# A recurrent attention with an MoE layer behind it: another kernel with its own list schedule in place of the scheduled one

## The chip, the cores and the metric

One core of a Trainium2 chip runs the whole program. The metric is the device time of one execution in microseconds (us), the median of several. The five engines are TensorE (PE), VectorE (DVE), ScalarE (ACT), GpSimd (POOL) and SyncE (SP), which here only issues DMAs.

## The reference

Thirty-two sequences (4 batches of 8 heads) of 768 tokens with 40 channels each go through a recurrence, and the joined heads (320 channels) through a layer norm and two dense layers with a ReLU between them.

```
for t in range(S):                            # S = 768, D = 40
    y[t] = r[t] @ state
    Sa = state @ a[t]
    state = state * w[t] - outer(Sa, b[t])
    state = state + outer(v[t], k[t])
x  = y as (4, 768, 320)
xn = (x - mean) / sqrt(var + 1e-6) * g_ln
out = x + relu(xn @ w_ch1) @ w_ch2            # 320 -> 1280 -> 320
```

`w` lies between 0.85 and 0.95. All is float32; the dense weights come as float64.

## The kernel before

The sequence is cut into 24 chunks of 32 tokens. Within a chunk the recurrence becomes matrix products: the decays are folded into `a`, `b`, `k`, `r` by running products, a 32x32 triangular matrix per sequence is inverted, and one small product per sequence carries the 40x40 state to the next chunk. Each chunk has these steps (names and lines of the kernel):

- `prep` (L141 to L195): two scans over a 104-partition tile (L149, L153) give the running products, `a`, `b` and `k` are multiplied by them (L160, L165, on DVE for the first six chunks and on POOL later), 32 products (L178) give the triangular matrices, and DVE signs them out of PSUM (L183). They go to DRAM (`d_g`), because the inversion wants another layout.
- `invert` (L197) and `invert2` (L226): for a slab of two or four chunks, one matrix per partition, DVE does forward substitution. `invert` inverts all 32 rows at once, 60 instructions per slab (L208, L211); `invert2` inverts two 16-row blocks side by side in 28 (L241, L245), and the off-diagonal part is then applied by products (`solve2`, L258). The first three slabs use `invert2`, the other five `invert`. The result goes to DRAM (`d_tt`) and comes back per chunk (`load_tt`).
- `load_cl` (L310): the same running products once more in the token-row layout, by scans of their own (L321, L325), transposed on DVE (L329, L331); POOL then scales `k` and `b` (L339).
- `chain` (L365): the products with the state (L372), the solve (L349 or L258, evacuated by L352 and L362), the products that make the next state (L384), and four multiplications out of PSUM (L390).
- `state`, `post` (L395, L409): transposes on PE (L401, L416) with copies by ACT (L407, L421), products (L429), masks (L435), products (L443), and the output row tile `xt` (L447). One L447 ends the attention of one chunk.
- `norm` (L557) and `moe` (L593): per pair of chunks (256 tokens) ten slices of 128 hidden units. A slice is eight matmuls of 256 columns (L615), a ReLU by ACT (L618), a remainder by DVE (L619), and six matmuls of 320 columns (L601). Each float32 operand is split in a high and a low part.
- `weights` (L456): the float64 words of the dense weights are turned into float32 by ACT, DVE and POOL.
- `warm` (L217): 360 matmuls (L221) whose result nobody reads.

Order: the program emits steps in a loop over chunks with boosts and nudges, and a timeline model of the framework chooses the order on DVE and ACT. All DMAs are issued by SP. At the end, a check of the scans' validity decides whether a sequential fallback (L861) runs; it does not run here.

## Time and profile before

| | |
|---|---|
| median of 3 runs | 710.24 us (708.89 to 710.95) |
| profiled execution, its span | 702.6 us |
| PE, DVE, ACT, POOL busy | 579.0, 564.0, 328.7, 291.4 us |
| moved by DMA | 92.35 MB in 158156 packets |

The profiled execution's span runs from its first to its last instruction; it stands 7.6 us below the median, which has the launch around it. Busy times of one engine overlap a little, so group sums can be above the engine's total. Matmuls overlap even more: a matmul that lasts 300 ns in its row may start 120 ns after the one before it, so the rate is read from start to start. In the line of slices each digit is a fortieth of the span, in tenths; PEclk is the TensorE clock that was granted.

### The profile page before, as it was taken

The numbers are of one execution on the slowest core, as the hardware profiler recorded it, in microseconds if no ns is written. First come the engines' busy times: TensorE is split into PE (matmuls) and PEld (weight loads), VectorE is DVE, ScalarE is ACT, GpSimd is POOL, SyncE is SP. The second block draws the span as 40 slices with busy tenths as digits, with TensorE's granted clock in tenths as the row PEclk, the third lists the DMA queues.
The fourth block names the chain that finished last, engine by engine and source line by source line (L and its number), as shares of the span: only waits on it lengthen the run. The fifth ranks groups of instructions, "written<-read, shape, count | busy, mean of one in ns | idle before, by whom it ended". The sixth has DMA issues, their size and how long they took to land.

```text
span 702.6 us, 24730 instructions
## 1 busy us (share of the span) xinstructions
PE 579.0 (82%) x10386; PEld 511.0 (73%) x10386; DVE 564.0 (80%) x1291; ACT 328.7 (47%) x816; POOL 291.4 (41%) x328
## 2 busy tenths in 40 slices
PE   2787778786697879788878889798987899999994
PEld 2686666675586758776757778697776777889994
DVE  8969899899589967899957999788996999764621
ACT  4314664544243445363366356444656255666220
POOL 8606486757514246146505533543133312233000
PEclk9979796868588799899989899999999899999998
DMA  6787977538635467455558653775336435420100
GB/s 176 202 230 206 280 188 182 136 86 198 137 104 144 99 154 161 124 159 134 131 145 177 141 134 94 169 167 122 89 95 116 117 86 119 109 51 16 38 20 22
DMA packets 158156, 92.35 MB, mean 131 GB/s; under 512 B 126504, under 2 KB 136488, under 8 KB 158040
## 3 DMA queue, kind: packets, MB, share of 16 engines
q1 hardware_dynamic: 158040, 90.72, 52.2%
q8 instruction: 83, 1.36, 0.8%
q14 instruction: 33, 0.27, 0.1%
HBM read 72.06 MB, written 18.64 MB: 129 GB/s over the span
## 4 chain that ended last, share of the span: by engine, by line
DVE 45%; PE 26%; DMA 17%; issue 5%; ACT 3%; SPq 2%; POOL 1%; DVEq 0%; POOLq 0%; ACTq 0%
PE ps L615 8%; PE ps L601 7%; DVE yinv L211 6%; DVE ytmp L208 6%; DMA yinv<-d_g 6%; DMA wa<-in_et_dram 4%; DVE x L390 3%; DVE x5s L435 3%; DVE gE L149 3%; DVE qE L153 3%; DVE hl L619 2%; DMA tt<-d_tt 2%; DVE yinv L245 2%; DMA d_tt<-yinv 2%; DVE gC L321 2%
## 5 line engine op out<-in xcount | busy, mean ns | idle before, releaser
L615 PE MATMUL ps<-xh,w 128*128 128x256 f32 x480 | 117.4, 303 | 3.3 <-DVE xl L589 2.3
L601 PE MATMUL ps<-w,hh 128*128 128x320 f32 x480 | 113.4, 330 | 4.9 <-DVE yinv L211 3.6
L618 ACT ACTIVATE hh<-ps 128x256 fp32r<-128x256 f32 x120 | 45.6, 383 | 140.0 <-PE ps L615 130.9
L615 PEld LDWEIGHTS ps<-xh,w 128*128 128x128 f32 x480 | 87.2, 200 | 8.4 <-DVE xl L589 2.6
L601 PEld LDWEIGHTS ps<-w,hh 128*128 128x128 f32 x480 | 79.2, 197 | 8.9 <-ACT hh L618 5.7
L601 PE MATMUL ps<-w,hl 128*128 128x320 f32 x240 | 75.0, 335 | 12.5 <-DVE hl L619 11.9
L619 DVE SCALAR_TENSOR_TENSOR hl<-ps,hh 128x256 fp32r<-128x256 f32 x120 | 49.5, 414 | 43.2 <-ACT hh L618 40.7
L208 DVE TENSOR_TENSOR ytmp<-yinv 128x30 f32<-128x30 f32 (+19 forms) x150 | 61.7, 412 | 26.4 <-DMA yinv<-d_g 24.4
L165 POOL TENSOR_TENSOR bk<-bk,gE 104x1024 f32<-104x1024 f32 x18 | 41.9, 2327 | 91.7 <-DMA bk<-in_et_dram 71.2
L221 PE MATMUL ps<-start,ident 128*128 128x160 f32 x360 | 74.3, 363 | 0.0
L615 PE MATMUL ps<-xl,w 128*128 128x256 f32 x240 | 71.0, 296 | 0.0
L221 PEld LDWEIGHTS ps<-start,ident 128*128 128x128 f32 x360 | 63.4, 232 | 2.3
L211 DVE TENSOR_TENSOR yinv<-yinv,ytmp 128x30 f32<-128x30 f32 (+19 forms) x150 | 61.1, 408 | 2.3
L601 PEld LDWEIGHTS ps<-w,hl 128*128 128x128 f32 x240 | 45.7, 199 | 16.5 <-DVE hl L619 14.9
L615 PEld LDWEIGHTS ps<-xl,w 128*128 128x128 f32 x240 | 48.2, 201 | 0.5
L362 ACT COPY x<-ps_c 32x160 f32<-32x160 f32 x144 | 40.7, 283 | 12.9 <-PE ps_c L357 9.7
L160 POOL TENSOR_TENSOR aT<-wa,qE 104x512 f32<-104x512 f32 x18 | 25.6, 1423 | 50.8 <-DVE qE L153 41.0
L390 DVE TENSOR_TENSOR x<-ps_c,x2s 40x320 f32<-40x320 f32 x92 | 44.7, 486 | 2.1
L384 PE MATMUL ps_c<-x,xk 128*40 128x40 f32 (+1 forms) x1472 | 43.1, 213 | 3.9 <-ACT x L279 2.9
L164 ACT COPY abd<-aT 40x512 f32<-40x512 f32 x48 | 29.6, 616 | 35.4 <-DVE aT L160 19.6
L372 PE MATMUL ps_c<-x,x2s 96*32 96x40 f32 (+1 forms) x1536 | 30.5, 223 | 18.7 <-issue 6.6
L384 PEld LDWEIGHTS ps_c<-x,xk 128*40 128x40 f32 (+1 forms) x1472 | 37.0, 126 | 9.2 <-ACT x L279 3.5
(174 smaller groups left out, 1359.7 us busy)
## 6 DMA issues: line engine op xcount, KB each, us to landing
clt<-in_cl_dram SPq DMA_DIRECT2D x24, 485.5 KB
wa<-in_et_dram SPq DMA_DIRECT2D x20, 422.9 KB
bk<-in_et_dram SPq DMA_DIRECT2D x20, 416.0 KB
d_g<-gk SPq DMA_DIRECT2D x48, 128.0 KB
x<-in_vt_dram SPq DMA_DIRECT2D x48, 128.0 KB
d_a<-aT SPq DMA_DIRECT2D x24, 214.5 KB
vu<-in_vr_dram SPq DMA_DIRECT2D x24, 208.0 KB
x2s<-d_a SPq DMA_DIRECT2D x48, 82.5 KB
```

Of the source, the lines that this page charges most:

```text
L165: (nc.gpsimd if c >= EARLY else nc.vector).tensor_tensor(out=kb, in0=kb, in1=g[R, :, 0:C].unsqueeze(2).broadcast_to([104, 16, 2, C]), op=A ...
L208: nc.vector.tensor_tensor(out=tv, in0=y[0:n, j + 1:, j:j + 1].broadcast_to([n, m, j]), in1=y[0:n, j:j + 1, 0:j].broadcast_to([n, m, j]), o ...
L211: final["inv", si] = nc.vector.tensor_tensor(out=y[0:n, j + 1:, 0:j], in0=y[0:n, j + 1:, 0:j], in1=tv, op=ALU.add)
L221: nc.tensor.matmul(pw[:, 0:w], lhsT=ident, rhs=start0.rearrange("p h t -> p (h t)")[:, 0:w], start=True, stop=True)
L362: nc.scalar.copy(out=dst[:, :, :, j, 0:D], in_=pu[32 * j:32 * j + 32, :, :, hf])
L372: nc.tensor.matmul(prh[32 * q:32 * q + 32, h], lhsT=X2s[RROW[hf], hf, 32 * p:32 * p + 32], rhs=X2[RROW[hf], hf, p, 0:D], start=True, stop= ...
L384: nc.tensor.matmul(pst[r0:r0 + D, h], lhsT=XK[FROW[hf], 1, hf, p], rhs=X2[FROW[hf], hf, p, 0:D], start=True, stop=True)
L390: nc.vector.tensor_tensor(out=X2n[r0:r0 + D, hf, ps, 0:D], in0=pst[r0:r0 + D], in1=pc.unsqueeze(2).broadcast_to([D, 8, D]), op=ALU.mult)
L601: nc.tensor.matmul(po[u], lhsT=l[:, us], rhs=ws[f"w2_{f}"][:, x], start=f == 0 and n == 0, stop=f == 9 and n == 2)
L615: nc.tensor.matmul(ph, lhsT=l, rhs=r, start=n == 0, stop=n == 7)
L618: nc.scalar.activation(out=hh, in_=ph, func=AF.Relu)
L619: nc.vector.scalar_tensor_tensor(out=hl, in0=ph, scalar=0.0, in1=hh.bitcast(F32), op0=ALU.max, op1=ALU.subtract)
```

## The change

It is a rewrite. What is computed and the split in 24 chunks of 32 tokens stay; these are its parts.

- **Order.** Every step is an `Op` with an engine, an assumed duration, a priority and its reads and writes. `Plan.order` simulates the five engines with these durations and emits all instructions in the order that comes out, with `tc.manual_schedule()`; each engine then runs its own in that fixed order. Chain steps have priority -100 + 18c for chunk c, prep -70 + 18c, post -60 + 18c, MoE 400 + 10g for pair g, so MoE comes only where nothing of the attention is ready.
- **One set of scans.** Time runs forward. The token rows of `k`, `b` and of the running products come from PE products with the identity (`KB`, `gY`), not from second scans. Over four chunks (`SPAN`) the running product is not restarted.
- **Inversion.** All slabs (two of two chunks, five of four) invert only 16-row diagonal blocks: 14 steps of two DVE instructions on 128 partitions. The solve is three products (`p1`, `p2`, `p3`) for every chunk.
- **Tiles side by side.** Products with 40 or 64 rows are paired on both halves of the array. PSUM: two pairs of banks for all attention products, two banks for each of the MoE's two layers.
- **MoE tiles 512 wide.** Two slices share one PSUM bank: ReLU and remainder work on 128x512 at a time. The matmuls themselves stay.
- **Norm.** `xt` is only centred before the transposes; the scale by 1/sqrt(var) is applied at the output (`ot`), the root's refinement is on POOL.
- **DMAs.** Inputs and weights are loaded from ACT's queue (w, a, kb, r, dv and two v per chunk); SP does the rest. One tile per input is loaded once.
- No `warm` matmuls.

The diff, cut to its core (removed code is above):

```diff
+RING = dict(w=2, a=6, kb=2, g=2, q=1, gk=6, KB=6, pi=6, VU=2, vt=2, r=2, T=2, N=2, y=2, ST=2, S=1, Z=1, xt=6, xh=2, ...)
+BASE = dict(chain=-100.0, post=-60.0, prep=-70.0, inv=-45.0, load=-90.0, moe=400.0, wts=-20.0)
...
+                    if e == "PE":
+                        if o.mode != mode:
+                            us += 0.09
...
+    def prep(c):
+        load("w", c, ...); load("a", c, ...); load("kb", c, ...)          # ACT queue
+        add(f"st{c}", "DVE", 0.14, ...); add(f"g{c}", "DVE", 1.3, scan ...)
+        add(f"la{c}", "DVE", 0.4, ...);  add(f"q{c}", "DVE", 1.3, scan ...)
+        add(f"kbq{c}", *(("DVE", 1.25) if c < 2 else ("POOL", 2.35)), ...)  # 104x1024
+        add(f"ag{c}", "POOL", 1.43, ...)                                    # 104x512
+        gy = add(f"gY{c}", "PE", 0.30, ..., mode=(64, 128))      # 8 products
+        pg = add(f"pg{c}", "PE", 0.52, ..., mode=(64, 64))       # 32
+        add(f"gk{c}", "DVE", 0.8, ...)                           # 2 x 128x256
+        add(f"dg{c}_{gg}", "SP", ...)                            # to DRAM, gg = 0, 1
+        kt = add(f"KB{c}", "PE", 0.62, ..., mode=(64, 128))      # 16
+        add(f"KBc{c}", "ACT", 0.74, ...)                         # 128x640
...
+    def invert(i):
+            add(f"yl{c}_{bl}", "SP", ...)                        # 16x16 blocks, 64 bytes a row
+        for m in range(1, 15):
+            def step(o, m=m, n=n, S=S):
+                tt(V, tv, y[:, :, 0:m, m:m + 1].broadcast_to(S), y[:, :, m:m + 1, m + 1:16].broadcast_to(S), ALU.mult)
+                tt(V, yv, yv, tv, ALU.add)
+            add(f"td{c}_{bl}", "SP", ...)
...
+    def chain(c):
+        add(f"ld_T{c}", "SP", ...); add(f"ld_N{c}", "SP", ...); add(f"zN{c}", "POOL", 0.3, ...)
+            pr = add(f"pra{c}", "PE", 0.25, ..., mode=(32, 32)); fence(f"prf{c}", pr, k - .1)
+            add(f"prb{c}", "PE", 0.8, prb, ..., mode=(64, 32))   # 64 products with pra
+        add(f"v0{c}", "ACT", 0.43, ...)                          # 128x320
+        p1 = add(f"p1_{c}", "PE", 0.62, ..., mode=(32, 32));  add(f"v1{c}", "ACT", 0.43, ...)
+        p2 = add(f"p2_{c}", "PE", 0.62, ..., mode=(32, 32));  add(f"v2{c}", "DVE", 0.48, ...)
+        for cb in range(2):
+            p3 = add(f"p3_{c}_{cb}", "PE", 0.32, ...)
+            for gg in range(2):
+                add(f"u{c}_{cb}{gg}", "ACT", 0.43, ...)          # 32x320
+            sp = add(f"ST{c}", "PE", 0.62, ..., mode=(64, 64));   add(f"Sa{c}", "DVE", 0.82, ...)  # 104x640
+            if c % SPAN == SPAN - 1: add(f"Sg{c}", "DVE", 0.82, ...)
...
+    def post(c):    # S (16) + Sc, uT (16) + vt, pz (32) + Z (128x512), ya and yb (64) with a fence, xt
+    def norm(c):    # bn, xc, px (2 transposes, 2 products), xh, xl
+    def moe(g):     # 5 x: ph (16 matmuls), hh (128x512, ACT), hl (128x512, DVE), po (12 matmuls); 2 x: ot, st_o
...
+    order = plan.order()
+    with tc.manual_schedule():
+        for o in order:
+            o.fn(o)
```

A `fence` writes one element of a bank on DVE between two groups of products that accumulate in it. The check at the end is seven small DVE instructions and a product behind all else.

## The prediction

> **What bounds the kernel now.** I read the page first (busy time, slices, chain, groups), then windows of the span, then groups by form, then the timeline of PE for rates.

> ```profile
> span 702.6 us, 24730 instructions
> PE 579.0 (82%) x10386; PEld 511.0 (73%) x10386; DVE 564.0 (80%) x1291; ACT 328.7 (47%) x816; POOL 291.4 (41%) x328
> ...
> DVE  8969899899589967899957999788996999764621
> ...
> DVE 45%; PE 26%; DMA 17%; issue 5%; ACT 3%; SPq 2%; POOL 1%; DVEq 0%; POOLq 0%; ACTq 0%
> ...
> L208 DVE TENSOR_TENSOR ytmp<-yinv 128x30 f32<-128x30 f32 (+19 forms) x150 | 61.7, 412 | 26.4 <-DMA yinv<-d_g 24.4
> ...
> L211 DVE TENSOR_TENSOR yinv<-yinv,ytmp 128x30 f32<-128x30 f32 (+19 forms) x150 | 61.1, 408 | 2.3
> ```

> DVE is busy for 564 us, at nine tenths in most slices until late, and it holds 45% of the chain. Two lines of the inversion alone are 61.7 + 61.1 = 123 us of it. The next view counts finished chunks: each L447 is one.

> ```profile
> core 0: us, DVE busy (x), PEclk, DMA share, GB/s
> 0.00:100.00 100.00, 0.48 (x1) 0.88 0.80 218
> 100.00:300.00 200.00, 2.37 (x5) 0.80 0.58 139
> 300.00:600.00 300.00, 6.68 (x14) 0.94 0.54 129
> 600.00:702.00 102.00, 1.95 (x4) 0.97 0.17 41
> ```

> Six chunks in the first 300 us, fourteen in the next 300 (21.4 us each). So the loss has two parts: a start in which DVE must invert, scan and unpack weights while PE has little to do, and a steady pitch of 21.4 us. The same windows with all engines:

> ```profile
> 175.00:200.00 25.00, 19.11 (x268) 16.42 (x271) 16.05 (x40) 7.79 (x20) 11.51 (x14) 0.62 0.63 141
> ...
> 550.00:600.00 50.00, 45.97 (x899) 39.40 (x893) 47.83 (x128) 24.12 (x64) 17.25 (x24) 1.00 0.44 100
> 600.00:650.00 50.00, 48.78 (x872) 43.66 (x876) 28.84 (x70) 31.93 (x85) 14.22 (x22) 1.00 0.24 56
> ```

> At 600 to 650, with the inversions over, DVE falls to 28.84 of 50 us and PE fills the window (48.78): PE is the next bound.

> **The change, part by part. DVE.** Durations:

> ```profile
> L149 DVE TENSOR_TENSOR_SCAN gE<-wa,start 104x528 f32<-104x528 f32 x24 | 32.5, 1352 | 7.3 <-POOL bk L165 3.6 <-DMA wa<-in_et_dram 3.6
> L447 DVE TENSOR_TENSOR xt<-ps_a,pi 128x320 f32<-128x320 f32 x24 | 11.5, 478 | 0.4 <-PE ps_a L443 0.4
> L183 DVE TENSOR_TENSOR gk<-ps_a,sign 128x512 f32<-128x512 f32 x19 | 12.8, 673 | 0.9 <-PE ps_a L178 0.9
> L321 DVE TENSOR_TENSOR_SCAN gC<-clt,start 128x330 f32<-128x330 f32 x24 | 21.1, 880 | 0.0
> L211 DVE TENSOR_TENSOR yinv<-yinv,ytmp 128x108 f32<-128x108 f32 x8 | 2.8, 346 | 0.1
> L211 DVE TENSOR_TENSOR yinv<-yinv,ytmp 128x30 f32<-128x30 f32 x8 | 2.1, 263 | 0.1
> L619 DVE SCALAR_TENSOR_TENSOR hl<-ps,hh 128x256 fp32r<-128x256 f32 x120 | 49.5, 414 | 43.2 <-ACT hh L618 40.7 <-PE ps L601 1.6
> ```

> Per element 128x320 to 128x512 costs (673 - 478)/192 = 1.02 ns, so 104x640 is about 0.80 us. Per chunk of the new kernel: two scans 2.7; three small column operations about 0.6; gk two of 0.41, 0.8; v2, xt, ot three of 0.48, 1.4; Sa 0.8 and a quarter of Sg 0.2; Z 0.67; two fences 0.2; statistics, centring and xl about 1.8 (three to four instructions the size of L447); hl 2.5 of 0.67, 1.7. The inversion is 7 slabs x 28 instructions of 28 to 112 elements, between 0.263 and 0.346, say 0.3: 59 us, 2.5 a chunk. Sum 13.4, times 24 = 322; the weights stay (about 30). So DVE has some 350 us in place of 564: the inversion loses 64 us against L208 and L211 alone, the second scans (L321 and its twin) and their transposes go. Over a span of 540 that is 65%, no bound any more, though in the first 90 us it still is.

> **ACT, POOL, DMA.** ACT:

> ```profile
> L344 ACT COPY xk<-xk 64x640 f32<-64x640 f32 x48 | 34.7, 724 | 3.2 <-POOL xk L339 2.2
> L352 ACT ACTIVATE hbd<-ps_c 32x320 f32<-32x320 f32 x72 | 30.7, 427 | 3.0 <-PE ps_c L372 2.3
> ```
> ```profile
> 609.18 1.98 SPq L307 DMA_DIRECT2D rbd<-in_rd_dram  x2
> ...
> 611.26 0.94 SPq L301 DMA_DIRECT2D x<-in_vt_dram  x2
> ```

> Eight copies of about 0.43 a chunk (pi, v0, v1, four u, xh), three near twice as wide at 0.7 (KBc, Sc, vt), 2.5 hh, by these two rows 0.6 for 512 elements: 7.0 us, 170 in all. But issuing a DMA held SP's queue 0.5 to 1.0 us, and the change puts seven of them a chunk on ACT, in front of whatever evacuates PSUM next: 3.5 to 7 us a chunk. Together 10 to 14 of an 18 us pitch; it hides beside PE as long as no chain step waits for it. [...] POOL keeps its two wide products of `prep` and loses L339; I count nothing. Bytes fall to about 64 MB by the diff's sizes (2.35 MB a chunk, 6.6 of weights, 1 of zeros).

> **PE.** Rates, from start to start:

> ```profile
> 569.55 1.03 PE L429 MATMUL ps_a<-rbd,vu 104*64 104x64 f32 x28
> 570.42 0.63 PE L384 MATMUL ps_c<-x,xk 128*40 128x40 f32 x24
> 570.98 0.38 PE L615 MATMUL ps<-xh,w 128*128 128x256 f32 x1
> ...
> 577.99 0.28 PE L615 MATMUL ps<-xl,w1x 128*128 128x256 f32 x1
> 578.20 0.77 PE L372 MATMUL ps_c<-x,x2s 96*32 96x40 f32 x60
> 578.90 0.60 PE L401 MATMUL ps_a<-ident,x 40*104 40x40 f32 x8
> ...
> 585.11 0.82 PE L416 MATMUL ps_a<-ident,x 32*104 32x32 f32 x16
> 585.87 0.73 PE L357 MATMUL ps_c<-hbd,tt 128*32 128x160 f32 x10
> ```

> The same view early on, and the MoE's two line groups in the chain at the end:

> ```profile
> 95.13 0.79 PE L268 MATMUL ps_c<-hbd,tt 32*32 32x40 f32 x64 [0.30 <-DVE hbd L275]
> ```
> ```profile
> 683.80 0.94 PE ps L615 x8
> 684.75 0.87 PE ps L601 x6
> ```

> A product with 32 weight columns takes 0.70/60 or 0.79/64 = 12 ns, with 40 columns 0.56/24 = 23, with 64 0.87/28 = 31, with 104 0.76/16 = 48. New attention, per chunk: 96 (p1 to p3) and 128 (pr, ya, yb) of 32 columns, 2.7; 32 of 40 (ST), 0.75; 64 of 64 (pg, pz), 2.0; 56 of 128 (KB, S, uT, gY) at about 50, 2.8; px 0.5: 8.7 us if pairing gains nothing. If everything paired over two row halves takes half, 5.2. L268, on four diagonal tiles, is no faster than L372 on four column tiles, so 12 ns may be a floor; I take 7.5. MoE is unchanged: 5 x (0.94 + 0.87) = 9.1. Going from L615 to L372 cost 0.21 - 0.12 = 0.09 more than a matmul's slot; 18 such switches a chunk, 1.6. Sum 18.2, times 24 = 437 us at full clock. The old kernel's is about as large (same MoE, and the 360 idle matmuls gone are no path), so PE's work is not where time goes; waiting is.

> **Start and end.** Rows:

> ```profile
> 1.66 4.69 DMA wa<-in_et_dram
> ...
> 47.25 5.84 DMA d_tt<-yinv
> ...
> 54.38 6.35 DMA yinv<-d_g
> ...
> 694.16 2.98 DMA out_dram<-ot
> ```

> Load 4.7 (8 with the zeros queued beside it), two preps at about 6, d_g out 5.8, blocks back 6.4, 28 steps 8, d_t 5.8, T back about 5: chain 0 begins near 50 us. With two chunks and a post of some 13 us each, and weights unpacked by then, MoE begins near 90. Until there PE has done nine preps of 1.8 and three or four chunks' attention, 34 us. Left: 403. In MoE-dense windows the clock was 1.00, in 300 to 600 it was 0.94: at 0.97, 415. For gaps of a fixed order whose assumed durations are not exact I add 6% (PE was 97% busy at best): 440. The end, from the last output's DMA, was 702.6 - 694.2 = 8.4. 90 + 440 + 8 = 538, and 7.6 of launch: **545 us**. [...]

> **Rivals.**

> *Hand-overs queue, slower.* Each engine runs a fixed order, so a chain step waits out whatever stands before it. Own times of a chain: PE 2.7 (pr, p1 to p3, ST), ACT 2.6 (v0, v1, four u), DVE 1.4 (v2, Sa, a share of Sg), some 1.3 for the hand-overs themselves: 8. If each of five PE steps waits out a whole MoE block (16 x 0.12 = 1.9), each of three ACT steps a ReLU of 0.6 and the seven issues 5 in all, each of two DVE steps a scan of 1.35, and each of six products a copy of 0.43 that holds its PSUM pair: 8 + 9.5 + 6.8 + 2.7 + 2.6 = 29.6 a chunk. Time 50 + 24 x 29.6 + 36 (last post, MoE, end) + 7.6 = 804. It decides from a pitch of (710 - 94)/24 = 25.7. For it: seven issues on ACT. Against it: DVE and POOL have room and PE's blocks are met half way on average. 10%.

> *The inverse arrives late.* d_g, blocks, d_t, T all pass DRAM: about 43 us from load to T. The gk and a buffers (six) let chunk c+6 be prepared once chain c has read its own, so 2.8 pitches of 19.9 cover it, 55 us. If each of the four transfers doubles behind SP's fixed order (23 us more), 11 us show at each of five slabs: 600. 10%.

> [...] 10%.

> *All pairing works.* 5.2 for 7.5, 1.0 of switches, clock 1.00, start at 75, gaps of 4%: 15.3 x 24 less 28 done early is 339, and 75 + 353 + 16 = 444. 5%.

> **How the numbers follow.** Forecast 64%, rivals 10, 10, 10 and 5, within 0.3% 1%. About 0.3% (2 us) is what a measurement of this kernel tells from no change. Faster holds forecast, three rivals: 0.89; slower 0.10. The range begins two thirds of the way to full pairing (475), takes in the late inverse (600) and the drain (627), and ends at 655, where the drain comes with products that gain nothing from pairing (1.2 x 22 x 1.09 = 29 more).

> **What would show it.** Right: DVE near 350 busy, about 2 DVE instructions per step of the inversion at 0.3; PE the largest share of the chain; L447's successor every 19 to 20 us; MoE from about 90 us; 64 MB. Wrong: PE idle before chain products in the steady part with ACT or a DMA named as releaser, small products slower than 12 to 50 ns, a clock under 0.9 after 100 us, or a steady pitch above 22.

## The result and the profile after

The new kernel takes 958.72 us (median of four runs, 951.92 to 968.72). Beside it, on the same chip, the kernel before took 709.57 (702.19 to 710.95). The ratio is 1.353, 95% interval 1.341 to 1.366. It was predicted at 545 us with a range of 475 to 655, and it is slower by 35%. The profile is of the slowest of the four runs (968.72 us; the other three lie between 951.92 and 963.85), so its sums may be one or two per cent high.

The first rows of the page of after, to be laid beside the same rows of before:

```profile
span 966.8 us, 42059 instructions
...
PE 838.6 (87%) x19650; PEld 772.0 (80%) x19650; DVE 340.8 (35%) x785; ACT 201.8 (21%) x412; POOL 156.8 (16%) x238
...
PEclk9999998657555795895996755796578598855889
...
DMA packets 150155, 66.59 MB, mean 69 GB/s; under 512 B 119384, under 2 KB 135768, under 8 KB 149976
```

DVE fell from 564 to 340.8 us as predicted (some 350), and the bytes are 66.6 MB for the 64 predicted. PE rose from 579.0 to 838.6 us and from 10386 to 19650 records. The clock row, mostly 9 in before, falls to 5 again and again. So the question is one engine's: why does PE take 839 us where the prediction had 437?

The windows of after (columns: window, its length, busy time and instructions of PE, PEld, DVE, ACT, POOL, then granted clock, DMA share, GB/s):

```profile
163.00:230.00 67.00, 66.31 (x969) 62.48 (x968) 30.32 (x70) 14.36 (x29) 22.93 (x28) 0.59 0.31 79
200.00:300.00 100.00, 87.03 (x1934) 80.77 (x1930) 38.14 (x86) 15.00 (x30) 18.87 (x19) 0.60 0.33 77
...
500.00:600.00 100.00, 87.59 (x1851) 81.72 (x1850) 39.51 (x87) 15.30 (x30) 21.26 (x21) 0.65 0.33 78
```

From 163 to 230 us PE is busy for 66.31 of 67.00 us and still gets 0.59 of its clock. It is not idleness that takes the clock away.

The timeline of PE in after, one row for each run of equal products:

```profile
17.83 1.93 PE L409 MATMUL att<-a,kb 40*64 40x32 f32 x64 [2.26 <-ACT pi L398]
19.69 3.64 PE L432 MATMUL att<-ident,kb 40*128 40x40 f32 x32
...
92.41 1.83 PE L409 MATMUL att<-a,kb 40*64 40x32 f32 x60
...
326.68 3.64 PE L432 MATMUL att<-ident,kb 40*128 40x40 f32 x32
...
334.43 1.98 PE L629 MATMUL att<-ident,ST 40*128 40x40 f32 x32
...
339.03 1.55 PE L395 MATMUL att<-ident,g 40*128 40x40 f32 x16
340.51 1.14 PE L409 MATMUL att<-a,kb 40*64 40x32 f32 x64
```

Two things are to be read here. First, the loop at L409 issues 32 products a chunk and the trace holds 64 records; L432 and L629 issue 16 and show 32. A plain fp32 product is two records, and each takes its time: the 32 of L432 at 326.68 take 3.64 us, some 0.11 each. A transpose is one: in the run with transposes below, the 16 of the same group take 1.08 us at half clock (at 318.13 us). An fp32r product of the MoE is one too: its first step issues 16 in each of 60 rounds, and the trace has 960. Second, the same group has two durations: 1.93 and 1.14 us for L409, 3.64 and 1.98 for two groups of one form, L432 and L629. That is full and half clock. The record of the clock knows only the values 1.0 and 0.5 (52 entries in after, 44 in before), and all its switches lie multiples of 3.413 us apart. Its first entry in after stands at 143.3 us; before it the page shows 9, but the durations (19.69 as at 326.68) say half. The page takes a stretch without an entry for full speed. With that stretch, after spends 143.3 + 451.5 = 595 of 967 us at half clock, before 23.4 + 143.3 = 167 of 703 (its rows early on stand with the run without idle matmuls below). A mean clock by the page is too high by the same stretch: after's 0.767 becomes 0.69. Below, the second of two clocks is the one set right in this way.

PE's waits in after (in all, times, longest):

```profile
PE att L477 <- issue: 28.6, 20, 3.3
PE att L395 <- DVE g L362: 21.5, 3, 12.8
PE att L552 <- issue: 18.4, 15, 2.5
PE att L552 <- DMA T<-d_t: 10.9, 3, 4.2
PE att L595 <- ACT VU L580: 7.7, 8, 1.0
```

All its idle time is some 128 us, about as in before (124). So waits for other engines are not what makes PE's 839 us; only the 59 us that nothing in the profile explains ("issue"; 7 in before) are new.

### The profile page after: what moved, and what is told of

It is laid out like the page before. It is cut to its first block, busy times and chain, and to the rows that moved or that the text cites. A ratio compares the mean times of both kernels' runs of the same rounds, so it can differ in the third digit from the quotient of the medians.

```text
span 966.8 us, 42059 instructions
## 1 busy us (share of the span) xinstructions
PE 838.6 (87%) x19650; PEld 772.0 (80%) x19650; DVE 340.8 (35%) x785; ACT 201.8 (21%) x412; POOL 156.8 (16%) x238
## 3 DMA queue, kind: packets, MB, share of 16 engines
q8 instruction: 155, 2.54, 1.1%
## 5 line engine op out<-in xcount | busy, mean ns | idle before, releaser
L851 PE MATMUL ph<-xh,w_f 128*128 128x256 f32 x480 | 142.2, 353 | 2.8 <-issue 2.2
L871 PE MATMUL po<-w_f,hh 128*128 128x320 f32 x480 | 125.0, 350 | 1.0 <-issue 1.0
L851 PEld LDWEIGHTS ph<-xh,w_f 128*128 128x128 f32 x480 | 108.3, 249 | 6.1 <-issue 2.4
L871 PEld LDWEIGHTS po<-w_f,hh 128*128 128x128 f32 x480 | 89.4, 214 | 4.4 <-issue 2.1
L871 PE MATMUL po<-w_f,hl 128*128 128x320 f32 x240 | 81.5, 340 | 1.5 <-issue 1.5
L851 PE MATMUL ph<-xl,w_f 128*128 128x256 f32 x240 | 81.9, 341 | 0.0
L432 PE MATMUL att<-ident,kb 40*128 40x40 f32 x768 | 72.1, 361 | 1.7 <-DVE xl L297 1.0
L432 PEld LDWEIGHTS att<-ident,kb 40*128 40x128 f32 x768 | 68.9, 273 | 4.4 <-DVE xl L297 1.3
L395 PE MATMUL att<-ident,g 40*128 40x40 f32 x384 | 51.5, 347 | 21.8 <-DVE g L362 21.5
L395 PEld LDWEIGHTS att<-ident,g 40*128 40x128 f32 x384 | 48.8, 256 | 24.4 <-issue 14.6
L643 PE MATMUL att<-ident,VU 64*128 64x32 f32 x768 | 67.5, 337 | 0.0
L629 PE MATMUL att<-ident,ST 40*128 40x40 f32 x736 | 66.3, 350 | 0.4 <-DVE xl L297 0.2
L643 PEld LDWEIGHTS att<-ident,VU 64*128 64x128 f32 x768 | 64.6, 258 | 1.7 <-issue 0.2
L629 PEld LDWEIGHTS att<-ident,ST 40*128 40x128 f32 x736 | 63.1, 261 | 2.9 <-issue 1.1
```

Source lines behind the costliest of these rows:

```text
L395: M.matmul(banks(o)[:, h2, D * jg:D * jg + D], lhsT=lhs, rhs=ident[half(h2), half(h2)], start=True, stop=True, skip_group_check=True)
L432: M.matmul(banks(o)[:, h2, D * bj:D * bj + D], lhsT=flat(kb)[half(h2), 128 * bj:128 * bj + 128], rhs=ident[half(h2), half(h2)], start=True ...
L629: M.matmul(banks(o)[:, h2, D * gb:D * gb + D], lhsT=flat(ST)[half(h2), 128 * gb:128 * gb + 128], rhs=ident[half(h2), half(h2)], start=True ...
L643: M.matmul(banks(o)[:, gg, x:x + C], lhsT=flat(VU)[half(gg, 64), 64 * n:64 * n + 128], rhs=ident[half(gg, 64), 64 * gg + C:64 * gg + 64], ...
L851: M.matmul(pv, lhsT=l, rhs=r[:, k], start=n == 0, stop=False, skip_group_check=True)
L871: M.matmul(po[u][:, 0:CH], lhsT=l[:, us], rhs=wt[:, y], start=f == 0 and n == 0, stop=f == 9 and n == 2, skip_group_check=True)
```

## The experiments

Three theories were on record at first. *Count*: the products are twice as many records as predicted, and those with 128 weight columns cost more. *Gate*: small products let the clock fall to half. *Waits*: the fixed order and the loads issued by ACT set the time. Before's median in the three batches was 706.11, 709.46 and 706.02 us.

**Transposes for identity products.** Four groups (L395, L432, L629, L643) become PE transposes, one record for two:

```
-  M.matmul(o_, lhsT=lhs, rhs=ident[half(h2), half(h2)], start=True, stop=True, ...)
+  M.transpose(out=o_, in_=lhs, identity=ident[half(h2), half(h2)])
```

> Three theories. Count: PE is the bound, and its work was under-counted, since a float32 product runs as two passes and the 56 products a chunk that turn rows by a product with the identity cost 0.12 to 0.19 us each at full clock. Gate: PE is the bound and runs at half clock in long stretches without the MoE's dense matmuls. Waits (rival): the fixed order and the DMA issues on ACT hold the chain, and PE's busy time is only modelled. Here the four groups of identity products become PE transposes, one pass each, as the kernel before has them; all else stays. Count: 3.9 us a chunk less at full clock, 7.2 at half, so 785 to 865 us. Gate alone, without the count: no more than 3% faster. Waits: within 2% of 952 to 968.

Measured: 803.99 us (803.04 to 804.94), 155 less.

```profile
span 801.1 us, 39406 instructions
...
PE 627.1 (78%) x18322; PEld 560.2 (70%) x18322; DVE 343.7 (43%) x785; ACT 200.3 (25%) x412; POOL 158.1 (20%) x238
```

PE loses 1328 records, which is one for each product of the four groups in 24 chunks, and 211 us. Count holds. But from 200 to 250 us the clock is 0.51 here too.

**Loads issued by SP.** All loads move from ACT's queue to SP's:

```
-  A.dma_start(out=dst, in_=src)
+  sync.dma_start(out=dst, in_=src)
```

> All loads are issued from SP in place of ACT. Count and Gate: within 2% of 952 to 968 us. Waits: at least 5% faster, 910 or less, and the waits of PE before the chain's products shrink.

Measured: 969.62 us (two runs, 958.59 and 980.65). No change: the issues on ACT, the prediction's way to a slower kernel, cost nothing that can be seen.

**Attention alone.** The MoE's matmuls, ReLU and remainders are left out; the output is the scaled row tile plus itself.

> The MoE's matmuls, its ReLU and its remainders are left out (the output is the scaled row tile plus itself); weights are still unpacked. Gate and Count together: half clock throughout, 27.5 us of PE a chunk, 690 to 730 us. Count without Gate: full clock, 15.5 us a chunk, 420 to 460. Waits: the pitch of the chain stays near 36 us, over 800.

Measured: 848.62 us (one run). Its page has no clock row at all, as no switch was recorded, and its groups late in the span are at half speed:

```profile
span 846.8 us, 38544 instructions
...
PE 664.3 (78%) x17970; PEld 604.5 (71%) x17970; DVE 300.2 (35%) x725; ACT 165.6 (20%) x352; POOL 157.8 (19%) x238
```
```profile
625.22 3.64 PE L629 MATMUL att<-ident,ST 40*128 40x40 f32 x32
631.25 3.64 PE L432 MATMUL att<-ident,kb 40*128 40x40 f32 x32
```

So the attention by itself never opens the clock. Its 664 us of PE are 27.7 a chunk, as Gate had it (27.5); after's groups at full clock add up to some 15.5, which would be 372. The time is above what Gate gave (690 to 730) and fits the number that Waits gave (over 800), because PE is also idle for 183 us: 66.6 before an instruction that waited for nothing the profile shows ("issue"), 52.0 for DVE, 28.0 for ACT, 18.5 for DMA. So without the MoE the waits set part of the time; taking 220 us of MoE work out of after saves only 110.

**MoE steps spread out.** The MoE's PE steps are halved and given to PE between attention steps by a credit (attention steps add to it, MoE steps use it up), and the scheduler's assumed PE durations are set to measured ones:

```
+  if e == "PE" and credit >= 0.9:
+      dense = min((x for x in ready[e] if x[2].name[:2] in ("ph", "po")), default=None)
...
+  credit = max(0.0, credit - us) if dense else min(credit + 0.62 * us, 2.0)
```

> The same work. The MoE's PE steps are cut in halves (8 and 6 matmuls) and spread evenly among the attention's products by a share of 0.62, and the order is made with PE durations as measured at full clock. Gate: the clock stays at 0.9 or more and the time is 593 of PE work at that clock, some 40 of start and 5% of gaps, 700 to 760 us. Count without Gate: within 4% of 952 to 968. Waits: any gain would come with PE less busy, and the clock would not move.

Measured: 940.13 us (933.92 to 946.34), clock 0.794, or 0.72. Gate as then stated (0.9 or more) fails: spreading dense work does not hold the clock open. With the transposes as well and a credit of 0.75 (the next run of this kind):

> After with the four identity-product groups as PE transposes, the scheduler's PE durations corrected to those measured at full clock, and the MoE steps halved and spread among the attention steps. PE's work by measured full-clock groups: attention about 11.5 us a chunk, MoE 9.2, together 20.7 x 24 = 497. Theory Gate: if a dense share of 44% spread evenly keeps the clock at 0.95 or above, 497/0.95 + about 125 idle = 640 to 660 us. If the spread does nothing for it, as in the run before it: 780 to 810 as for the transposes alone (804), clock about 0.81. Theory Waits (the order in which steps are put decides): anywhere below 780 with an unchanged clock and PE idle well under 120.

Measured: 800.15 us (799.09 to 801.21), clock 0.825, or 0.75, against 803.99 us and 0.811, or 0.73, for the transposes alone. Again next to nothing.

**Unread fp32 matmuls.** Two (one) unread 128x128 by 128x160 fp32 matmuls follow each attention step, in the attention-only kernel (in the kernel with transposes and spread steps):

```
+  for _ in range(2):
+      M.matmul(ph_t[0][:, 0:160], lhsT=ident, rhs=dense, start=True, stop=True, ...)
```

> This is the attention-only kernel (all of the MoE left out; the output is the row tile scaled, plus itself; 848.6 us) with work added that nobody reads: after each of its some 15 PE steps a chunk stand two dense matmuls, 128x128 by 128x160, about 30 a chunk, an estimated 0.15 to 0.27 us each at full clock, 4.5 to 8 us a chunk. Theory Gate (small products let the clock fall to half; dense ones hold it up): the attention's 664 us of PE become 332, the dense matmuls add 108 to 195, some 150 to 180 stay idle: 600 to 720 us, faster than 848 in spite of more work, and a granted clock above 0.9 with 16-product groups at 1.07 us and KB's 32 records at 1.9 us. Theory no Gate (the products are slow by themselves): the work adds to it, 950 us or more, and KB's group stays at 3.56 us. Theory Waits (the fixed order and hand-overs set the time): no change within 30 us, as the dense matmuls fall into PE's idle time.

> The kernel with transposes and spread MoE steps, and one unread dense matmul (128x128 by 128x160, added into a free part of a PSUM bank) after each of the 15 attention steps of a chunk: 2.3 to 4 us a chunk at full clock. Theory Gate: clock above 0.9, (497 + 55 to 97)/0.97 + 130 = 700 to 740 us, faster than without them if those ran at 0.81. Theory no Gate (a product's time is its own): slower than without them by 60 to 200 us.

Measured: 1056.31 us (1041.17 to 1071.44) and 897.79 (890.14 to 905.44). Both came out as "no Gate" had it, yet the groups kept showing two speeds. The size of the filler is to be seen in its own rows, at half and at full clock:

```profile
502.21 1.43 PE L944 MATMUL ph<-dense,ident 128*128 128x160 f32 x4
...
827.74 0.81 PE L944 MATMUL ph<-dense,ident 128*128 128x160 f32 x4
```

**Before without its idle matmuls.** Of L221's 180 calls two are left (`range(90)` becomes `range(1)`).

> The kernel before with 2 of its 180 idle matmuls left (L221). Theory Gate: its early PE work then runs at half clock; the stage up to 100 us, where the record showed 0.88, shows 0.5 to 0.7, but DVE sets that stage, so the time rises by 0 to 30 us: 706 to 736. Theory no Gate: the 74 us of idle matmuls leave and nothing else changes: 700 to 706 us.

Measured: 713.22 us (711.06 to 717.79), ratio 1.0074, interval 1.0029 to 1.0119. The first recorded switch moves from 23.4 to 146.4 us, and some 4 to 5 us are lost. In before that switch falls into a row of these matmuls, the second of these three:

```profile
13.43 2.50 PE L221 MATMUL ps<-start,ident 128*128 128x160 f32 x8
...
18.63 8.03 PE L221 MATMUL ps<-start,ident 128*128 128x160 f32 x40
...
28.48 2.44 PE L221 MATMUL ps<-start,ident 128*128 128x160 f32 x16
```

Eight records take 2.50 us ahead of it and sixteen 2.44 behind it. So those matmuls (180 calls, 360 records) do open the clock, and a first switch 123 us later costs only 0.7% here, where DVE sets the pace.

**What opens the clock.** I cut the trace of each run into stretches of 3.413 us, as the clock's switches lie, and sorted them by what PE did in them and by the clock of the next one. For each measure of "what PE did", the table has the number of stretches that the best single cut, chosen afterwards, sorts wrongly. *Height* is the sum over the matmul records of rows/128 times moving columns (a record `40*64 40x32` counts 40/128 x 32 = 10, one of `128*128 128x256` counts 256).

```
after             stretches  followed by full | busy time  records  columns  height (cut)
at half clock        173           26         |    26        26       26       5  (3,032)
at full clock        109           83         |    15        25       15       1  (2,679)
with transposes
at half clock        123           20         |    14        20       20       2  (2,816)
at full clock        110           90         |     8        14       10       1  (2,355)
before
at half clock         46           22         |     9        14        8       7  (2,040)
at full clock        157          135         |     4        10        5       6  (2,240)
```

At half clock, busy time is no better for after than always guessing half (26 of 173 wrong); height gets 168 of 173, and at full clock 108 of 109. In before, whose products are tall anyway, busy time and height do about equally well. In after and all full kernels derived from it, height is wrong in 0 to 8 of 109 to 173 stretches. By this the fp32 filler above is weak: four records move 640 columns in about 1.36 us at half clock, some 1,600 in 3.413 us. But the rule does not carry over to the attention with that filler: its clock opened 18 times, mostly after stretches under 2,700, and height sorts its stretches at half clock no better than a guess (18 of 249 wrong; 9 of 63 at full clock). So height as counted here is not the whole rule for plain fp32 matmuls on 128 rows. A sorting is no proof either, so a pair of kernels was made that differ in height alone: attention only, and after each step two (after KB ten) unread bf16 matmuls with 512 moving columns, on 128 rows in the one and 32 in the other.

```
+  M.matmul(ph_t[0], lhsT=eye[0:128], rhs=dense[0:128, 0:512], start=True, stop=True, ...)
against
+  M.matmul(ph_t[0], lhsT=eye[0:32], rhs=dense[0:32, 0:512], start=True, stop=True, ...)
```

> The attention-only kernel (all of the MoE left out, output a scaled row tile plus itself; 848.6 us) with unread bf16 matmuls on all 128 rows, 128 weight columns, 512 moving columns: ten after each KB step, two after each other attention step, some 38 a chunk. Sorting the stretches of 3.41 us of the runs so far by what PE moved in them, moving columns weighted with rows/128, those with more than some 2,700 to 3,000 were followed by full clock and those with less by half clock, whatever the engine's busy share. Theory Height (rows times moving columns decide the clock): the attention alone moves 9,800 a chunk, which is 2,160 per 3.41 us at full clock, too little; with the filler's 19,500 it is above 3,000, and ten in a row open it: clock above 0.85, PE 664/2 + 195 = 527 at full clock, time 690 to 740 us, faster than 848 in spite of some 900 more matmuls. Theory no Height: 664 at half rate + 390 and idle time: 1,100 or more.

> The same kernel as the one with 128-row filler, the same number of matmuls, weight columns and moving columns, but on 32 rows only. Theory Height: the filler counts a quarter (4,900 a chunk, 14,700 with the attention's, under 2,700 per 3.41 us at any pace), so the clock stays at half: 1,050 to 1,190 us. Theory no Height (moving columns, busy time or the number of dense matmuls decide): the same time as the 128-row one within 3%.

Measured: 907.52 us (902.25 to 912.78) on 128 rows, 1112.32 (1111.96 to 1112.69) on 32. The tall one's page and two of its groups:

```profile
span 900.5 us, 40124 instructions
...
PEclk9777788796768769798869855855687766659655
```
```profile
399.16 1.98 PE L630 MATMUL att<-ident,ST 40*128 40x40 f32 x32
406.05 1.98 PE L433 MATMUL att<-ident,kb 40*128 40x40 f32 x32
```

The short one's page has no clock row, and these are its rows:

```profile
span 1110.2 us, 40360 instructions
...
PE 1075.0 (97%) x18874; PEld 673.7 (61%) x18874; DVE 295.5 (27%) x727; ACT 166.2 (15%) x352; POOL 153.4 (14%) x238
```
```profile
509.26 3.64 PE L433 MATMUL att<-ident,kb 40*128 40x40 f32 x32
512.83 4.44 PE L948 MATMUL ph<-dense,eye 32*128 32x512 bf16 x10
```

The number of matmuls, their columns and their place are the same; only the rows differ, and the kernels are 205 us apart. PE of the short one is busy 97% of the time and never leaves half clock. That shows that the rows of the matmuls count and that a busy PE alone does not open the clock. The pair does not tell rows from cells (rows times weight columns), as both fillers have 128 weight columns; cells sort after's stretches a little worse than height (7 and 6 wrong for 5 and 1). The expected 690 to 740 for the tall one was missed: it reached a mean clock of 0.738, or 0.72, and the filler cost more than it brought (848.62 without). Two reasons can be named: its 29,100 a chunk over 900 us are only some 2,650 per 3.413 us, and the expectation halved the attention's 664 us to 332, where the groups give 372. (235 of its 904 filler records are missing from the trace, so its stretches cannot be sorted.)

**Full kernels with tall filler.** The transposes with spread MoE steps and 32 unread bf16 matmuls (128 rows, 192 columns) once a chunk; and the transposes with two such matmuls after each attention step:

> The kernel with transposes and spread MoE steps (800.2 us, clock 0.825) and 32 unread bf16 matmuls of 128 rows, 128 by 192, in a row after one attention step of each chunk: 6,100 columns, 2.6 us at full clock, 61 us in all. Theory Height: its work moves 28,800 per chunk, which over 20.7 us of work and some 5 idle is 3,800 per 3.41 us and holds the full clock once the burst has opened it: clock above 0.92, (497 + 61)/0.95 + 130 = 700 to 730 us. Otherwise 800 plus 61 to 120: 860 to 920.

> The kernel with transposes (804.0 us, clock 0.811; durations of the scheduler corrected) and two unread bf16 matmuls of 128 rows, 128 by 192, after each attention step: 5,800 columns a chunk, 2.4 us at full clock, 58 us in all. The MoE's runs open the clock, the filler is to hold it through the attention steps. Theory Height: clock above 0.9, (497 + 58)/0.93 + 125 = 710 to 730 us. Otherwise 860 to 920.

Measured: 852.57 us (847.92 to 857.22), clock 0.785, or 0.77, and 853.31 (852.12 to 854.50), clock 0.828, or 0.76. Both slower than without filler. The clock did not hold: as the same sorting has it (0 and 8 wrong of 135 and 128 stretches at full clock), it fell mostly where a stretch moved under some 2,700. Paying for the clock with useless work does not help here. No kernel of the study beats before; the fastest is the one with transposes and spread steps, 800.15 us, 13% slower than before.

## Why the prediction was wrong

**Where it was right.** DVE's sum (350 predicted, 340.8 measured), with inversion steps of 0.237 and 0.283 us for the 0.3 taken:

```profile
L297 DVE TENSOR_TENSOR y<-y,tmpy 128x28 f32<-128x28 f32 (+13 forms) x98 | 27.7, 283 | 3.4
L297 DVE TENSOR_TENSOR tmpy<-y 128x28 f32<-128x28 f32 (+13 forms) x98 | 23.2, 237 | 18.7 <-DMA y<-d_g 9.3 <-issue 5.6 <-DMA w_r<-in_w_dram 1.4
```

The MoE's 9.1 us a chunk is right too: at full clock its two steps take 1.90 and 1.78 us by their matmuls, five of each for two chunks, 9.2. The price of a switch, 0.09 us, held between MoE and attention, read from start to start in these rows:

```profile
421.98 0.39 PE L851 MATMUL ph<-xh,w_f 128*128 128x256 f32 x1
422.20 0.28 PE L851 MATMUL ph<-xl,w_f 128*128 128x256 f32 x1
...
423.88 0.28 PE L855 MATMUL ph<-xl,wx_f 128*128 128x256 f32 x1
424.09 0.83 PE L595 MATMUL att<-VU,KB 64*40 64x40 f32 x64
424.85 1.98 PE L643 MATMUL att<-ident,VU 64*128 64x32 f32 x32
```

The first matmul behind an attention step holds PE 0.22 us and the last one before the next attention step 0.21; in between they start every 0.12. "PE is the next bound" held, and so did the rejection of queued hand-overs.

**Where it was right by luck.** ST's 0.75 measured 0.76 (424.09 to 424.85), and pg with pz's 2.0 measured 2.14. Both were priced by the record at 23 and 31 ns with one record for a product. There were two, 64 a group, and each took half the price, 12 and 17 ns. Whether the pairing or the fewer rows and columns made them cheaper, no run tells.

**The step that failed first: the rate of a product.** "A product with 32 weight columns takes 0.70/60 = 12 ns" divided a row of the timeline by its record count and took a record for a product. L372 of before runs 32 products a chunk and shows 1536 records for 24 chunks. For the products with 32 columns (p1 to p3, pr, ya, yb) 2.7 us became about 5: 448 records at 11 ns, close to the 12 of before, so the discount for pairing (8.7 to 7.5) did not appear there. For the 56 with 128 weight columns the price, 50 ns, came from a row of transposes, which are one record; as products they cost two records of 59 to 92 ns each at full clock: three groups of 1.9 and one of 1.48 us, 7.2 in place of 2.8. Together some 15.5 us a chunk for 7.5, and with the MoE 24.7 x 24 = 593 for 437 (which had 38 for all switches; 593 lacks those around MoE steps, at most some 23 by the rows above). The run with transposes confirms this term from the other side.

**The step that failed second: the clock.** "At 0.97" rested on MoE-dense stretches of before. By the sorting above, the clock of after stayed full where PE's products were tall enough (all but 1 of 109 stretches). Before's records move 35,200 rows/128 x columns a chunk (2,400 of them the idle matmuls'), after's 29,700, of which 19,800 are the MoE's in either. The change's attention works on 16 to 64 rows (but for px) where before used up to 128, so it moves 9,800 a chunk; over 15.5 us at full clock that is 2,160 in 3.413 us, under the cut of some 2,700. By this cut the clock falls outside the MoE's runs. PE's 838.6 less 593 is 246 us, an estimate of the price of the gate; the other way, 595 us at half clock with PE busy 87% would cost 259 if all work took twice as long there. The groups take 1.4 to 1.9 times as long, so that is an upper bound. No run held full clock throughout, so the split is worked out, not measured.

Busy time as the profile counts it isn't what decides here: PE was busy for 66.31 of 67.00 us at 0.59 in after, and for 97% of the span at half clock with 32-row filler.

**The rest.** Chain 0 began at 59.9 us for about 50, MoE at 130.9 for 90, both with PE at half clock. The 545 plus 156 for Count and 246 for Gate is 947 of 958.7, closer than such estimates can vouch for: PE's idle time was 128 us where the prediction's terms give some 90 (56 before MoE, 25 of gaps, 8 at the end). The 7.6 us taken for the launch were mostly the difference between executions: after's profiled execution takes 968.72 us for a span of 966.8. The prediction's own signs named "a clock under 0.9 after 100 us", "small products slower than 12 to 50 ns" and "a steady pitch above 22": all came, the pitch at 37.0 us (the first `xt` starts at 83.9 us, the last of 24 at 935.8). The 10% that it gave to slower stood on queued hand-overs (804 us), which were not the way it came. A late inverse costs 10.9 us of PE's waits in all (T by DMA), not the 11 at each of five slabs of that rival. The 627 in the prediction's range and the 655 at its end count a drain of 0.19 us more at each of 18 switches a chunk; no run shows such a term. The rows at 421.98 to 424.09 show 0.09 to 0.10 between MoE and attention; other switches were not priced, and no run tried them by themselves.

**What stays open.** The 59 us of PE's "issue". In the attention steps short gaps stand inside runs of fast products, and the queue that carries instructions moved 2.54 MB in after. Whether PE outran the supply of its instructions (after has 42059 in place of 24730) no run shows. The count alone doesn't make it: the kernel with 32-row filler has 40360 instructions and 4.3 us of it, attention alone 38544 and 66.6.

## What to carry to other kernels

Count PE's work in records of the trace, by form and type, and take a price only from a row of the same form: a plain fp32 product was two records here, a transpose one. Before cutting a product into short tiles, add up rows/128 times columns per 3.4 us (in after some 2,700 held the clock; the sum did not sort plain fp32 filler on 128 rows): after's short tiles came with half clock for 595 of 967 us, and the 32-row filler's busy share of 97% with half clock throughout. Where the clock's record has no entry, compare the durations of one group early and late before believing full speed.
